# Gated attention in half chunks of 64 tokens with a middle state, four shared PSUM banks and a new order of the work

## The chip, the core and the metric

The kernel runs on one core of a Trainium2 chip. The core has five engines that work side by side, each strictly in its own order: TensorE multiplies matrices (its weight loads have a row of their own in the trace, PEld), VectorE (DVE) does elementwise work, ScalarE (ACT) applies functions and copies, GpSimd (POOL) and SyncE (SP) mostly issue transfers. TensorE writes its results to PSUM, which has eight banks of 2 KB in each of 128 partitions. The metric is the device time of one execution in microseconds, as the median of several.

## What is computed

For each of 4 x 8 heads a state of 48 x 48 complex numbers runs through 768 tokens: it is multiplied by a complex decay for each token and row, the outer product of `k` and `v` is added, and the output is `q` times its real part. A feed-forward block follows.

```python
def _attn_ref(q, k, v, a_re, a_im):
    ...
    for t in range(S):
        ar, ai = (a_re_n[:, :, t, :, None], a_im_n[:, :, t, :, None])
        new_re = ar * S_re - ai * S_im
        new_im = ar * S_im + ai * S_re
        kv = np.einsum('bhd,bhe->bhde', k[:, :, t], v[:, :, t])
        S_re, S_im = (new_re + kv, new_im)
        y[:, :, t] = np.einsum('bhd,bhde->bhe', q[:, :, t], S_re)

def _moe_ref(x, w_in, w_out):
    h = x @ w_in
    g = h * (1.0 / (1.0 + np.exp(-h)))
    return g @ w_out
```

`x` is the attention's output as 3072 x 384, `w_in` is 384 x 2048 and `w_out` 2048 x 384. The decay's size is capped at 0.999.

## The kernel before

The tokens are cut into 24 chunks of 128, numbered `n` from 0 to 23: four batches by six places in the sequence. Chunk `n` hands its state on to chunk `n + 4`, and the last four chunks hand on nothing. Two chunks form a pair `p`, twelve in all, and a pair's 256 tokens go through the feed-forward block together.

The recurrence of a chunk is done with matmuls. Two running sums over its tokens (`phases`, `summed`; in the order below `phase:n` and `L:n`) give the angle and the logarithm of the decay; sine, cosine and exponential follow on ScalarE. VectorE multiplies `k` and `q` by decay and rotation (`K`, `Q`), so that each head has 96 rows, a real and an imaginary part of 48. They are turned so that these 96 lie on the partitions: `squared` (`tk`, `tq`) transposes blocks of 32 x 32 on VectorE, and `homed` (`td`) moves the blocks home with 12 transfers, six on SP's queue and six on POOL's, into the tile `T`. Then per chunk:

- `weights` (`w:n.0`, `w:n.1`, line 613): for each head the product of all 128 keys with all 128 queries, four heads to a bank, into `a`.
- `masked` (`m`, line 626): VectorE multiplies each of the two banks with a triangle of ones, so that a query sees no later key, and writes `w`.
- `output` (`y:n`, lines 645 and 648): for each head the masked products times `v`, and from chunk 4 on `q` times the state `S`, added up in one bank. A head has 48 columns of weights but 64 are loaded, and even and odd heads go to the lower and the upper 64 partitions.
- `put` (`x:n`, lines 689 and 693): ScalarE copies the bank to `xT` and the last part of it to `y3`.
- `state` (`s:n`, line 716 from chunk 6 on): the chunk's own sum of `k` times `v`. It lies the wrong way round, so `state_squared` (`ss`, line 723) transposes it in blocks into `ssq` and `state_homed` (`sd`, line 734) moves it home with 12 transfers. `carried_on` (`S`, lines 749 and 751) adds the old state, multiplies by the whole chunk's decay `dec` and hands the result on.

The feed-forward block is `hidden` (`h:p.j`, lines 766, 776, 783), `silu` (`g`), the split of its result into parts (`gr`, `gb`, `gc`) and `result` (`r:p.j`, lines 968, 986, 1004). Its weights stand in three parts whose products make up for a lower precision; some parts are read again from memory for each pair (`lv`, `lw`).

A list of about 2,000 words such as `y:6` sets the order: each word is one step, and the steps' instructions go to their engines in that order. Nothing is reordered afterwards. PSUM has two banks for `phase`, `L`, `a`, `y` and `s` in turn, two for `h` in turn, and four for the block's results `o`.

## Time and profile before

| | |
|---|---|
| median of 3 runs | 606.78 us (606.25 to 607.14) |
| span of the profiled execution | 603.4 us |
| TensorE, matmuls | 583.3 us, 97% of the span |
| TensorE, weight loads | 509.3 us, 84% |
| VectorE | 495.7 us, 82% |
| ScalarE | 441.2 us, 73% |
| POOL | 222.5 us, 37% |

The span reaches from the first instruction of the program to the last; what lies around it makes up the difference to the run's time. Busy times of different engines overlap. A matmul's end is modelled, so what one costs is read from the starts of the records that follow each other, not from its duration. An fp32 matmul leaves two records.

### The profile page before, as it was taken

To read this page: it belongs to the slowest core of one execution; us is meant where nothing else is said; L and a number is where in the kernel's file an instruction comes from. 1 tells how busy PE (TensorE), PEld (TensorE's weight loads), DVE (VectorE), ACT (ScalarE), POOL (GpSimd) and SP (SyncE) were. 2 spreads that over 40 slices of the span, in tenths; PEclk is the share of its full clock that TensorE was granted. 3 is DMA by queue.
4 is the path that set the end of the run, shared out by engine and by line. 5 is a ranking of instruction groups with operands and counts; after the bars stand their busy time and mean duration, and the time that the engine had idled before them with its cause. 6 is when DMAs were issued, how large, how long until landed. Compare 5 with 4: busy or idle time off the path is not lost. (4 is left out here: it accounts for less than half of the span.)

```text
span 603.4 us, 11507 instructions
## 1 busy us (share of the span) xinstructions
PE 583.3 (97%) x3828; PEld 509.3 (84%) x3828; DVE 495.7 (82%) x765; ACT 441.2 (73%) x695; POOL 222.5 (37%) x389
## 2 busy tenths in 40 slices
PE   8588999999999999999999999999999999999997
PEld 6367877787767998998898898998898898999996
DVE  5899999987998989989889888889878786654644
ACT  7999999889885698896898895897884552342332
POOL 6364543636231534554444441536720323000000
PEclk9589999999999999999999999999999999999999
DMA  8988688977869977777868777859768467445652
GB/s 177 253 186 197 181 195 185 224 195 174 224 206 265 216 187 185 161 152 209 193 162 210 162 158 204 174 147 211 151 169 245 141 183 205 147 155 172 210 184 83
DMA packets 167728, 112.23 MB, mean 186 GB/s; under 512 B 137724, under 2 KB 143424, under 8 KB 167664
## 3 DMA queue, kind: packets, MB, share of 16 engines
q1 hardware_dynamic: 151920, 89.69, 57.2%
q0 software_dynamic: 12288, 17.23, 14.4%
q10 hardware_dynamic: 3456, 4.52, 2.1%
q8 instruction: 32, 0.52, 0.4%
q14 instruction: 32, 0.26, 0.2%
HBM read 81.14 MB, written 11.47 MB: 153 GB/s over the span
## 5 line engine op out<-in xcount | busy, mean ns | idle before, releaser
L307 ACT ACT_TABLE_LOAD x69 | 88.5, 1283 | 2.3 <-ACT ot L1017 0.8
L313 ACT ACTIVATE g<-h 128x512 f32<-128x512 f32 x96 | 56.0, 593 | 46.0 <-PE h L783 23.9
L600 POOL DMA_DIRECT2D T<-sq x120 | 70.1, 609 | 31.1 <-PE a L613 10.6
L944 ACT ACTIVATE head<-g 128x512 fp32r<-128x512 f32 x75 | 47.2, 630 | 46.2 <-PE o L986 25.9
L888 DVE SCALAR_TENSOR_TENSOR tail<-g,head 128x512 fp32r<-128x512 f32 x75 | 51.3, 683 | 32.1 <-ACT head L944 16.7
L528 POOL DMA_DIRECT2D dec<-ends x48 | 32.7, 722 | 117.6 <-DMA ends<-eq 116.8
L986 PE MATMUL o<-coarse,head 128*128 128x384 f32 x256 | 57.1, 344 | 0.5 <-ACT ot L1017 0.5
L766 PE MATMUL h<-xL,fine 128*128 128x512 f32 x192 | 55.3, 396 | 0.4 <-DMA fine<-w_firsts 0.4
L766 PE MATMUL h<-xD,mixed 128*128 128x512 f32 x192 | 55.2, 396 | 0.4 <-DVE xD L892 0.3
L986 PE MATMUL o<-diff,gd 128*128 128x384 f32 x256 | 55.4, 337 | 0.0
L892 DVE TENSOR_TENSOR gd<-tail,g 128x512 fp32r<-128x512 f32 x75 | 51.5, 687 | 4.3
L734 POOL DMA_DIRECT2D S<-ssq x84 | 46.8, 601 | 16.2 <-DVE ssq L723 10.3
L613 PEld LDWEIGHTS a<-T 96*128 96x128 f32 x384 | 49.9, 196 | 2.6 <-ACT T L605 0.3
L613 PE MATMUL a<-T 96*128 96x128 f32 x384 | 51.7, 281 | 0.1
L986 PEld LDWEIGHTS o<-coarse,head 128*128 128x128 f32 x256 | 44.8, 188 | 4.1 <-issue 1.1
L986 PE MATMUL o<-fine,tail 128*128 128x384 f32 x224 | 48.0, 336 | 0.0
L986 PEld LDWEIGHTS o<-diff,gd 128*128 128x128 f32 x256 | 45.5, 188 | 0.2 <-DVE gd L892 0.2
L776 PE MATMUL h<-xT,w 128*128 128x256 f32 x192 | 43.7, 381 | 1.6 <-ACT xT L689 1.6
L766 PEld LDWEIGHTS h<-xD,mixed 128*128 128x128 f32 x192 | 35.7, 188 | 10.1 <-DVE xD L892 1.2
L766 PEld LDWEIGHTS h<-xL,fine 128*128 128x128 f32 x192 | 36.0, 188 | 9.4 <-DMA fine<-w_firsts 0.8
L968 PE MATMUL o<-w,g 128*128 128x384 f32 x128 | 43.5, 488 | 0.0
L776 PEld LDWEIGHTS h<-xT,w 128*128 128x128 f32 x192 | 36.0, 190 | 7.9 <-ACT xT L689 1.8
(182 smaller groups left out, 1400.1 us busy)
## 6 DMA issues: line engine op xcount, KB each, us to landing
fine<-w_firsts SPq DMA_DIRECT2D x40, 384.0 KB
diff<-w_diffs SPq DMA_DIRECT2D x40, 384.0 KB
T<-sq SPq DMA_DIRECT2D x120, 64.0 KB
T<-sq POOLq DMA_DIRECT2D x120, 64.0 KB, 3.6
small<-in_moe_w_in_dram SPq DMA_DIRECT2D x16, 384.0 KB
raw<-in_moe_w_out_dram SPq DMA_DIRECT2D x16, 384.0 KB
small<-in_moe_w_out_dram SPq DMA_DIRECT2D x16, 384.0 KB
raw<-in_moe_w_in_dram SPq DMA_DIRECT2D x24, 192.0 KB
```

Of the source, the lines that this page charges most:

```text
L307: nc.scalar.preload_act_table_set(SETS[of][0])
L313: nc.scalar.activation(out=out, in_=in_, func=func, **kw)
L600: (nc.gpsimd if a % 2 else nc.sync).dma_start(out=to[ts(b, Q), :, a], in_=X[n]["sq"][ts(a, Q), b].rearrange("p w h x -> p (w h) x"))
L613: nc.tensor.matmul(ps[:, h], lhsT=x["kT"][hh * HH + h], rhs=x["qT"][hh * HH + h], start=True, stop=True)
L734: (nc.gpsimd if g % 2 else nc.sync).dma_start(out=to[ts(b, Q), r, :, e], in_=sq[ts(g, Q), :, b, 0:e.stop - e.start])
L766: nc.tensor.matmul(ps, lhsT=w[:, dc, ts(p % 2, C)], rhs=x[:, :, dc], start=(f == 0 and dc == 0), stop=(f == len(forms) - 1 and dc == ND - 1))
L776: nc.tensor.matmul(ps[:, ji], lhsT=of_first(w1, dc, jp * 2 + ji), rhs=A[p]["xT"][:, dc], start=(dc == 0), stop=(dc == ND - 1))
L888: nc.vector.scalar_tensor_tensor(out=dst, in0=whole, scalar=MORE / FINER, in1=head.bitcast(F32), op0=ALU.mult, op1=ALU.subtract)
L892: nc.vector.tensor_tensor(out=dst, in0=tail, in1=whole, op=ALU.subtract)
L944: nc.scalar.mul(g_form(p, jp, "head"), A[p]["g", jp], MORE * SPLIT / FINER)
L968: nc.tensor.matmul(A[p]["o"][m].rearrange("p n c -> p (n c)"), lhsT=A[p]["g", jp][:, ji, ts(m, C)], rhs=w2[jp][:, ji], start=(j == 0), sto ...
L986: nc.tensor.matmul(A[q_]["o"][m].rearrange("p n c -> p (n c)"), lhsT=left[:, i, ts(m, C)], rhs=right, start=(first_ and n == 0), stop=(las ...
```

## The change

From chunk 6 on (`n >= FULL`) a chunk is treated as two halves of 64 tokens.

- `weights_in_halves` (`wa`) forms only the two blocks on the diagonal, 64 keys by 64 queries: 16 matmuls for 8, each with half the weight columns and half the moving columns. The halves go to the lower and upper 64 partitions, so all eight heads fit one bank, and one mask on VectorE (`ma`) replaces two.
- What queries of the second half see of the first half comes from a state in the middle of the chunk. `state_of_pairs` now forms a sum for each half, over 64 tokens, into two banks. Both are transposed (`ss`) and moved home (`sd`), 12 transfers of twice the size, into a tile `new` with a single buffer. `middle` (`Sm`) adds the old state to the first sum on VectorE. The last four chunks need the first sum alone, where they had none before.
- `output` becomes two steps: `output_of_states` (`ys`) multiplies `q` of the first half by `S` and `q` of the second half by the middle state; `output_of_values` (`yv`) adds the masked products times `v`, contracting over 64 tokens. Each half has a bank of its own. `put` copies from two banks.
- `carried_on` adds both sums and writes the new state over the old one. `ssq` takes the buffer of `qr`.
- The running sum for `L` is no longer halved by its matrix; the exponential halves it by its scale.
- Four banks are shared by all users but `o`: each step takes the bank that was given back longest ago.
- The order is a new one throughout, not only where steps were replaced.

```diff
+class Banks:
+    def __init__(self, pool, n):
+        self.pool, self.free, self.of = pool, list(range(n)), {}
+    def tile(self, shape, dtype, *, name):
+        b = self.free.pop(0)
+        t = self.pool.tile(shape, dtype, tag=f"bank{b}", name=name, bufs=1)
+        self.of[name] = b
+        return t
+    def give(self, name):
+        self.free.append(self.of.pop(name))
...
-    p_m = Ring(fast.enter_context(tc.tile_pool(name="p_m", bufs=1, space=PSUM)), 2)
-    p_h = Ring(fast.enter_context(tc.tile_pool(name="p_h", bufs=1, space=PSUM)), 2)
+    banks = Banks(fast.enter_context(tc.tile_pool(name="p_b", bufs=1, space=PSUM)), 4)
...
+    def weights_in_halves(n):
+        x = X[n]
+        ps = banks.tile([C, H, SUB], F32, name=f"a{n}")
+        for h in range(H):
+            for i in range(2):
+                nc.tensor.matmul(ps[ts(i, SUB), h], lhsT=x["kT"][h][:, ts(i, SUB)],
+                                 rhs=x["qT"][h][:, ts(i, NA // 2)], start=True, stop=True)
+        x["a"] = ps
...
+    def outputs(n, left, right):
+        ps, first = output_banks(n)
+        for hp in range(HH):
+            for i in range(2):
+                for r in range(2):
+                    h = 2 * hp + r
+                    m = 64 if h + 1 < H else D
+                    nc.tensor.matmul(ps[i][64 * r:64 * r + m, hp], lhsT=left(i)[:, ds(h * D, m)],
+                                     rhs=right(i, h), start=first and hp == 0,
+                                     stop=not first and hp == HH - 1)
...
+    def output_of_states(n):
+        x = X[n]
+        s = [t.rearrange("p h d -> p (h d)") for t in (x["S"], x["new"][:, 0])]
+        outputs(n, lambda i: s[i], lambda i, h: x["qT"][h][:, ts(i, NA // 2)])
...
+    def output_of_values(n):
+        x = X[n]
+        outputs(n, lambda i: x["all v"][ts(i, SUB)], lambda i, h: x["w"][ts(i, SUB), h])
...
     def state_of_pairs(n):
-        ps = p_m.tile([C, HH, D2], F32, tag="m", name=f"s{n}")
-        for h in range(H):
-            hp, r = divmod(h, 2)
-            nc.tensor.matmul(ps[64 * r:64 * r + 64, hp], lhsT=x["all v"][:, ds(h * D, 64)],
-                             rhs=x["kr"][:, h].rearrange("p c d -> p (c d)"),
-                             start=True, stop=True)
+        x["ps"] = [banks.tile([C, HH, D2], F32, name=f"s{n}_{i}") for i in range(sums_of(n))]
+        for hp in range(HH):
+            for i, ps in enumerate(x["ps"]):
+                for r in range(2):
+                    h = 2 * hp + r
+                    nc.tensor.matmul(ps[64 * r:64 * r + 64, hp],
+                                     lhsT=x["all v"][ts(i, SUB), ds(h * D, 64)],
+                                     rhs=x["kr"][ts(i, SUB), h].rearrange("p c d -> p (c d)"),
+                                     start=True, stop=True)
...
+        new = X[n]["new"] = att.tile([D2, 2, H, D], F32, tag="new", name=f"new{n}", bufs=1)
...
+    def middle(n):
+        x = X[n]
+        mid = x["new"][:, 0]
+        nc.vector.tensor_tensor(out=mid, in0=mid, in1=x["S"], op=ALU.add)
...
-                v:8 turn:9 G5:5 g:1.7 ws:0 w:7.0 m:7.0 x:6 w:7.1 wk:3 wk:2 m:7.1 G1:5 wk:0 k:9 tk:8
...
+                phase:9 yv:6 x:6 hl:9 r:0.5 ul:9 ends:8 ws:3 K:8 wd:4 Sm:7 wq:5 wd:5 wk:3 G0:5 g:1.7
+                q:8 wa:7 wq:6 ma:7 last:8 k:9 ws:5 lv:2.0 r:0.6 wd:6 ys:7 yv:7 dq:8 x:7 G5:5 r:1.6
```

Three places show how instructions move. The first is TensorE at chunk 7. Before, `a` of the chunk is followed at once by its output; `T_1668` is the chunk's `T`, `S_829` its state, and the output's pattern goes on for 14 more rows:

```order
L648 MATMUL y_1722<-T_1455,S_756 48x128
L613 MATMUL a_0_1748<-T_1668 128x128 x4
L613 MATMUL a_1_1759<-T_1668 128x128 x4
L645 MATMUL y_1779<-w_0_1753,v_1327 64x128
L648 MATMUL y_1779<-T_1668,S_829 64x128
```

In the changed kernel it reads as follows, from the end of `ys` of chunk 6 (`T_1410`) to the start of `ys` of chunk 7 (`T_1637`); `new_1559` and `new_1711` are their middle states, in the same buffer:

```order
L681 MATMUL y_1_1684<-T_1410,new_1559 48x64
L483 MATMUL phase_1736<-th_parts_1611,upto_r 128x384 x2
L681 MATMUL y_0_1683<-w_1554,v_1404 64x64 x2
...
L1055 MATMUL o_0_943<-w_5_93,g_5_1439 128x384 x2
L1055 MATMUL o_1_944<-w_5_93,g_5_1439 128x384 x2
L656 MATMUL a_1793<-T_1637 64x64 x16
L1055 MATMUL o_0_943<-w_6_94,g_6_1607 128x384 x2
L1055 MATMUL o_1_944<-w_6_94,g_6_1607 128x384 x2
L681 MATMUL y_0_1826<-T_1637,S_767 64x64 x2
L681 MATMUL y_1_1827<-T_1637,new_1711 64x64 x2
```

The two `ys` are a phase, `yv` of chunk 6, two steps of `result` and `wa` of chunk 7 apart.

The second place is VectorE at the same point of the changed kernel: L819 is `middle`, L830 and L836 are `carried_on`, L663 is the mask.

```order
L819 TENSOR_TENSOR new_1559<-new_1559,S_708 96x384
L936 SCALAR_TENSOR_TENSOR fine_1701<-coarse,w_1_89 128x768
L979 TENSOR_TENSOR diff_1703<-coarse,mixed 128x768
L830 TENSOR_TENSOR new_1559<-new_1559 96x384
L836 TENSOR_TENSOR S_708<-new_1559,dec_1280 96x384
...
L936 SCALAR_TENSOR_TENSOR fine_1776<-coarse,w_4_92 128x768
L819 TENSOR_TENSOR new_1711<-new_1711,S_767 96x384
L936 SCALAR_TENSOR_TENSOR fine_1780<-coarse,w_5_93 128x768
L663 TENSOR_TENSOR w_1811<-a_1793,halves 128x512
```

Before, VectorE does the two masks of chunk 7 here in a row, and the state of chunk 6 is carried on some thirty rows later:

```order
L892 TENSOR_TENSOR diff_1746<-coarse,mixed 128x768
L626 TENSOR_TENSOR w_0_1753<-a_0_1748,upto_r 128x512
L626 TENSOR_TENSOR w_1_1766<-a_1_1759,upto_r 128x512
L594 STREAM_TRANSPOSE sq_1775<-kr_1634 128x3x4x2x32
L849 SCALAR_TENSOR_TENSOR fine_1777<-coarse,w_4_95 128x768
```

So the state's sums moved ahead of the masks and into the chain from chunk to chunk. On SP's queue the six transfers of chunk 7's sums stand between two stores of `w_diffs`, with a load of `q` and then `k` and `fine` behind:

```order
L1006 DMA w_diffs<-diff_1703 128x768
L813 DMA new_1711<-ssq_1675 32x8x32 x6
L1006 DMA w_diffs<-diff_1726 128x768
L547 DMA ends<-eq_1653 1x384
L1006 DMA w_diffs<-diff_1772 128x768
L197 DMA q_1791<-in_q_dram 128x8x48
```

The third place is ScalarE early on, ahead of the third and fourth copy into `xT`. Before:

```order
L307 ACT_TABLE_LOAD
L313 ACTIVATE mag_662<-mag_662 128x768
L605 COPY T_697<-tp_0_788 96x512
L307 ACT_TABLE_LOAD
L313 ACTIVATE g_1_814<-h_1_712 128x512
L248 ACTIVATE r<-raw 128x384
L307 ACT_TABLE_LOAD
L313 ACTIVATE eq_866<-L_833 128x384
L313 ACTIVATE L_865<-L_833 128x384
L248 ACTIVATE r<-raw 128x384
L307 ACT_TABLE_LOAD
L313 ACTIVATE g_0_872<-h_0_777 128x512
```

In the changed kernel, from the last table load ahead of the same copies:

```order
L324 ACT_TABLE_LOAD
L330 ACTIVATE g_0_816<-h_0_619 128x512
L330 ACTIVATE g_2_826<-h_2_819 128x512
L330 ACTIVATE g_3_837<-h_3_802 128x512
L263 ACTIVATE r<-raw 128x384 x3
L330 ACTIVATE g_1_871<-h_1_727 128x512
L330 ACTIVATE turn_893<-phase_878,round_b 128x384
```

Steps that need the same table now stand together. Up to the fourth copy into `xT` there are 12 table loads before and 8 now; on the path that runs, 70 before and 62 now.

## Rows read from the trace of the kernel before

**Rows 1.** The page's first part: busy us, share of the span, instructions.

```profile
PE 583.3 (97%) x3828; PEld 509.3 (84%) x3828; DVE 495.7 (82%) x765; ACT 441.2 (73%) x695; POOL 222.5 (37%) x389
```

**Rows 2.** Long stretches: length, busy PE, PEld, DVE, ACT, POOL, clock, DMA share, GB/s.

```profile
0.00:60.00 60.00, 45.75 (x305) 35.05 (x306) 50.80 (x98) 55.47 (x90) 32.23 (x58) 0.86 0.91 204
60.00:165.00 105.00, 105.00 (x653) 82.93 (x652) 96.14 (x151) 94.75 (x144) 49.38 (x77) 1.00 0.79 196
165.00:195.00 30.00, 29.14 (x144) 21.08 (x143) 27.90 (x37) 21.38 (x34) 8.00 (x14) 1.00 0.82 234
195.00:525.00 330.00, 329.54 (x2218) 296.75 (x2218) 279.66 (x416) 245.39 (x387) 132.93 (x240) 1.00 0.75 182
```

**Rows 3.** Timeline of TensorE, 307 to 314 us, merged: start, us, what.

```profile
307.53 2.04 PE L613 MATMUL a<-T 96*128 96x128 f32 x16
309.32 0.94 PE L986 MATMUL o<-coarse,head 128*128 128x384 f32 x4
310.10 0.86 PE L986 MATMUL o<-fine,tail 128*128 128x384 f32 x4
310.81 0.86 PE L986 MATMUL o<-diff,gd 128*128 128x384 f32 x4
311.59 0.88 PE L716 MATMUL s<-kr,v 128*64 128x96 f32 x16
312.30 0.44 PE L645 MATMUL y<-w,v 128*64 128x128 f32 x4
312.52 0.44 PE L648 MATMUL y<-T,S 96*64 96x128 f32 x4
...
313.85 0.44 PE L648 MATMUL y<-T,S 96*64 96x128 f32 x4
314.21 0.44 PE L986 MATMUL o<-coarse,head 128*128 128x384 f32 x1
```

**Rows 4.** The same from 311.5 us on: the last record ahead of `s`.

```profile
311.33 0.33 PE L986 MATMUL o<-diff,gd 128*128 128x384 f32 x1
```

**Rows 5.** Timeline of TensorE from 180 us: `s` without `y` behind it.

```profile
180.31 0.88 PE L716 MATMUL s<-kr,v 128*64 128x96 f32 x16
181.12 1.21 PE L613 MATMUL a<-T 96*128 96x128 f32 x8
```

**Rows 6.** Timeline of TensorE from 345.4 us: last `a` record, then `y`.

```profile
345.22 0.28 PE L613 MATMUL a<-T 96*128 96x128 f32 x1
345.44 0.43 PE L645 MATMUL y<-w,v 128*64 128x128 f32 x3
```

**Rows 7.** Timeline of VectorE at the same place, 343 to 347 us.

```profile
344.60 0.69 DVE L626 TENSOR_TENSOR w<-a,upto_r 128x512 f32<-128x512 f32 x1 [0.50 <-PE a L613]
345.54 0.69 DVE L626 TENSOR_TENSOR w<-a,upto_r 128x512 f32<-128x512 f32 x1 [0.25 <-PE a L613]
```

**Rows 8.** Groups by line and shape: busy us, mean ns, then idle time before.

```profile
L307 ACT ACT_TABLE_LOAD x69 | 88.5, 1283 | 2.3 <-ACT ot L1017 0.8 <-ACT ot L1011 0.4
L968 PE MATMUL o<-w,g 128*128 128x384 f32 x128 | 43.5, 488 | 0.0
L689 ACT COPY xT<-y 128x384 f32<-128x384 f32 x24 | 11.4, 473 | 17.9 <-PE y L648 17.6 <-PE h L776 0.2
L723 DVE STREAM_TRANSPOSE ssq<-s 128x384 f32<-128x384 f32 x14 | 8.1, 577 | 1.8 <-PE s L716 1.7
L693 ACT COPY y<-y 112x128 f32<-112x128 f32 x20 | 5.4, 270 | 0.0
L749 DVE TENSOR_TENSOR S<-S,S 96x384 f32<-96x384 f32 x14 | 7.6, 544 | 0.0
```

**Rows 9.** Line 734, the transfers of the sums: duration min/median/max, and landing.

```profile
L734 POOL DMA_DIRECT2D S<-ssq x84: 548/550/1170, 137.3 to 431.0; - x84
DMA to landing us min/median/max: 1.7/3.6/5.6
```

More of the change, by code (lines that the diff above doesn't have):

```diff
@@ L282 @@
     keep(ones, [[1, C]], 0, -1)
-    upto_r, half_r = (consts.tile([C, C], F32R, name=x) for x in ("upto_r", "half_r"))
+    upto_r = consts.tile([C, C], F32R, name="upto_r")
     nc.gpsimd.tensor_copy(out=upto_r, in_=ones)
-    nc.gpsimd.tensor_scalar(out=half_r, in0=ones, scalar1=0.5, scalar2=None, op0=ALU.mult)
-    upto, half = upto_r.bitcast(F32), half_r.bitcast(F32)
+    upto = upto_r.bitcast(F32)
+    halves = consts.tile([C, SUB], F32, name="halves")
+    for i in range(2):
+        nc.gpsimd.tensor_copy(out=halves[ts(i, SUB)], in_=ones[ts(i, SUB), ts(i, SUB)])
     one_b = consts.tile([C, 1], F32)
@@ L470, in phases @@
         x = X[n]
-        ps = p_m.tile([C, DM], F32, tag="m", name=f"phase{n}")
+        ps = banks.tile([C, DM], F32, name=f"phase{n}")
         running(ps, n, "th", upto, upto_r)
@@ L483, in turn @@
                                        op0=ALU.subtract, op1=ALU.add)
+        banks.give(f"phase{n}")
     def heads(t):
@@ L505, in summed @@
         first = n < STRAIGHT
-        ps = (p_o if first else p_m).tile([C, DM], F32, tag="o" if first else "m", name=f"L{n}")
-        running(ps, n, "l", upto if n < 2 else half, half_r)
+        ps = (p_o.tile([C, DM], F32, tag="o", name=f"L{n}") if first else
+              banks.tile([C, DM], F32, name=f"L{n}"))
+        running(ps, n, "l", upto, upto_r)
         x["L"] = ps
@@ L519, in decays @@
         x["decay"] = x["eq"]
-        special(x["eq"], x["L"], AF.Exp)
-        special(x["ek"], x["L"], AF.Exp, scale=-1.0)
+        whole = 1.0 if n < 2 else 0.5
+        special(x["eq"], x["L"], AF.Exp, scale=whole)
+        special(x["ek"], x["L"], AF.Exp, scale=-whole)
+        if n >= STRAIGHT:
+            banks.give(f"L{n}")
     def ends_of(n):
@@ L627, in masked, with masked_in_halves, output_banks @@
                                 in1=upto.unsqueeze(1).to_broadcast([C, HH, C]), op=ALU.mult)
+        banks.give(f"a{n}_{hh}")
+    def weights_in_halves(n):
[6 more added lines that the diff above has]
+        x["a"] = ps
+    def masked_in_halves(n):
+        x = X[n]
+        x["w"] = att.tile([C, H, SUB], F32, tag="w", name=f"w{n}", bufs=2)
+        nc.vector.tensor_tensor(out=x["w"], in0=x["a"],
+                                in1=halves.unsqueeze(1).to_broadcast([C, H, SUB]), op=ALU.mult)
+        banks.give(f"a{n}")
+    def output_banks(n):
+        x = X[n]
+        first = "y" not in x
+        if first:
+            x["y"] = [banks.tile([C, HH, SUB], F32, name=f"y{n}_{i}") for i in range(2)]
+        return x["y"], first
+    def outputs(n, left, right):
+        ps, first = output_banks(n)
+        for hp in range(HH):
+            for i in range(2):
+                for r in range(2):
[9 more added lines that the diff above has]
+    def output_of_values(n):
+        x = X[n]
+        outputs(n, lambda i: x["all v"][ts(i, SUB)], lambda i, h: x["w"][ts(i, SUB), h])
     def output(n):
@@ L688, in put @@
         ps = X[n]["y"]
-        nc.scalar.copy(out=A[p]["xT"][:, :, ts(i, C)], in_=ps[:, 0:ND])
-        if n >= STRAIGHT:
-            if "y3" not in A[p]:
-                A[p]["y3"] = att.tile([64 + D, T], F32, tag="y3", name=f"y3_{p}", bufs=1)
-            nc.scalar.copy(out=A[p]["y3"][:, ts(i, C)], in_=ps[0:64 + D, ND])
+        if n >= STRAIGHT and "y3" not in A[p]:
+            A[p]["y3"] = att.tile([64 + D, T], F32, tag="y3", name=f"y3_{p}", bufs=1)
+        parts = [(ps, ts(i, C), f"y{n}")] if n < FULL else [
+            (ps[k], ts(2 * i + k, SUB), f"y{n}_{k}") for k in range(2)]
+        for of, at, name in parts:
+            nc.scalar.copy(out=A[p]["xT"][:, :, at], in_=of[:, 0:ND])
+            if n >= STRAIGHT:
+                nc.scalar.copy(out=A[p]["y3"][:, at], in_=of[0:64 + D, ND])
+            banks.give(name)
     def state(n):
         x = X[n]
-        if place(n)[1] == NCH - 1:
-            return
         if n >= FULL:
@@ new lines @@
+                L:4 exp:4 v:3g k:4g F: F: H: H: q:5g k:6g s:3 S:3 R: t:3.1 J: J: G3:2 G6:2 G9:2 G8:2
+                im:6g thirds:3 q:4g w:2.1 t:3.2 T:3.2 h:0.3 T:3.1 m:2.1 Ga:2 H: g:0.0 h:0.2 g:0.2
+                dk:4 F: carried:4 w:3.0 g:0.3 im:7g ends:4 H: w:3.1 carried:5 m:3.0 R: J: m:3.1 H:
+                R: R: J: F: F: g:0.1 dq:4 L:5 re:7g phase:4 y:3 rd:4 turn:4 re:6g F: F: trig:4 K:4
+                y:2 last:4 phase:5 Q:4 x:3 H: tq:4 tk:4 J: r:0.0 R: R: x:2 G0:3 G5:3 J: H: J: G1:3
```

335 lines of the change are left out of this document (170 added, 165 removed).

## The prediction

> **What bounds the kernel now.** I began with busy time by engine: TensorE 97% of the span, VectorE 82%, ScalarE 73% [rows 1]. An average hides stages, so next came four long stretches [rows 2]. From 60 to 525 us TensorE is busy for all but 0.9 + 0.5 us; whatever its instructions take there is the time of the kernel. In the first 60 us it is busy for only 45.75, while ScalarE is busy for 55.47: there the end is set by ScalarE and VectorE, which prepare the first chunks. From 195 to 525 us VectorE has 279.66 of 330 us, 85%, so it has 50 us of room, but it works strictly in its order. A merged timeline of TensorE then gives the prices. One fp32 matmul leaves two records, so eight heads of `a` are 16 records.
>
> **TensorE's work before**, for chunks 6 to 23, the eighteen that change. `a` takes 1.79 us, from 307.53 to the next group at 309.32; `y` takes 1.91, from 312.30 to 314.21 [rows 3]. `s` takes 0.71 where `y` follows (311.59 to 312.30) [rows 3] and 0.81 alone (180.31 to 181.12) [rows 5]; of 14 chunks with an `s`, 6 have `y` behind it. Going from full-width to half-width weights costs 0.08: 311.33 to 311.59 is 0.26, where such a record takes 0.71 / 4 = 0.18 [rows 3, 4]. Coming back costs 0.14: the last four `y` records take 0.36 to the next group where others take 0.22 [rows 3]; this lies inside the 1.91 and the 0.81. The old order goes in 24 times. Sum: 18 x 1.79 + 18 x 1.91 + 6 x 0.71 + 8 x 0.81 + 24 x 0.08 = 32.2 + 34.4 + 10.7 + 1.9 = 79.2 us.
>
> **Its work after.** Four `y` records with 64 weight columns and 128 moving columns start over 0.22 us, so two of them, in the two column halves of the array, share 0.11 us [rows 3]. A full-width `a` record with 128 moving columns costs 1.79 / 16 = 0.11 by itself. Column halves therefore run side by side, at 0.00086 us per moving column; `s` with 96 columns fits (8 pairs x 0.083 = 0.66 of its 0.71). With 64 moving columns a pair should cost 0.055; I take 0.057. The upper bound is the 0.089 that a pair of `s` costs whole, since a load of 64 weight columns is hidden at 96 columns and no row shows it hidden at 64.
>
> `wa` and `ys`: 18 x 2 x 16 pairs x 0.057 = 32.8 us.
>
> `yv` and `s` now contract over 64 tokens, so two row halves and two column halves can hold four matmuls. No row before has a half of the rows. Side by side, `yv` is 18 x 8 fours at 0.055, 7.9 us; one row half after the other it is 288 pairs at 0.057, 16.4. I take 0.066 a four, 9.5 us, near the first, because column halves did run side by side and the two row halves write to different banks. `s` is 14 x 8 fours and 4 x 8 pairs (the last four chunks had no `s` before): 11.9 us at 0.083, 21.1 without row halves; taken 12.5.
>
> Switches: the new order enters half-width work 34 times, 34 x 0.22 = 7.5 us. Inside these runs it goes 21 times between half columns and quarters. No row shows that; between 0 and 0.22 each I take 0.14, 2.9 us.
>
> Sum 65.2, so **14.0 us less work**; bounds 20 less (0.055, fours side by side, free inner switches) and 33 more (0.089 for each pair, no row halves). [...]
>
> **What lies beside it.** VectorE: one mask of 0.69 us [rows 7] in place of two, 18 x 0.69 = 12.4 us less; 18 more transposes of 0.577 and 18 additions for the middle state at 0.544 [rows 8], 20.2 us more; net 8 us, within its 50 us of room. ScalarE: each chunk has two pairs of copies in place of one; from 0.473 for 384 and 0.270 for 128 columns [rows 8] half sizes cost 0.321 and 0.220, 18 x 0.34 = 6.1 us more. Against that the new order has 62 table loads for 70 on this path, 8 x 1.283 = 10.3 us less [rows 8]. Both are hidden by TensorE after 60 us. The last four chunks add 6 transfers on each of POOL's and SP's queues, 24 x 0.55 = 13 us of issuing [rows 9]; POOL is busy for 133 of 330 us there [rows 2], so I cost them at nothing beside the chain below. Shared banks remove no wait after 60 us, since there was none to speak of.
>
> **The start.** Up to the fourth copy into `xT` the new order has 8 table loads where the old has 12: 5.1 us of ScalarE in a stretch that ScalarE fills to 55.47 of 60 us [rows 2, 8]. VectorE is not relieved there (50.80 of 60). Between 0 and 6 us of TensorE's idle time can go; I take 3.
>
> **New waits.** *Chunk 7.* The buffer `new` is single and the state `S` is updated in place. So the sum of chunk 6 (`S:6`) waits for `ys:6` on TensorE, the transfers `sd:7` wait for `S:6`, the middle state `Sm:7` for the transfers, and `ys:7` for that. Price: 0.32 us from TensorE to VectorE (last `a` record at 345.22, its mask at 345.54) [rows 6, 7], two operations 1.1, six issues x 0.55, landing 3.6 [rows 9], addition 0.55 [rows 8], back 0.15: 9.0 us. Between `ys:6` and `ys:7` TensorE has a phase 0.36, `yv` 0.5, two results of four records at 0.340 [rows 8], `wa` 0.9, and three switches 0.66: 5.1 us. So TensorE waits 3.9 us. Behind `sd:7` on SP's queue stand the stores of `w_diffs` and the loads of `k`, `q` and `fine`; they are needed later than that. Elsewhere the same chain has 8.5 us (22 to 23), 9 (14 to 15, 18 to 19) or over 11 us of other work between; 0 to 3 each in the three short ones.
>
> *Masks.* Of the old kernel's masks the first starts while the second half of `a` runs, and `y` begins 0.22 us after the last `a` record has started [rows 6]. Now the one mask starts when all of `wa` is done: 0.32 + 0.69 + 0.15 (a mask ends at 345.29, `y` starts at 345.44) = 1.16 us, against 0.91 + 0.08 of `ys` between them. Seven chunks (9, 10, 13, 17, 19, 20, 23) have only `ys` there: 0.2 us each if VectorE stands ready, up to 0.9 more behind another operation. I take 3 us (1.4 to 7.7). The other chain waits, and VectorE at a few per cent more load over less time, together 3 us (0 to 8).
>
> **Sum.** -14.0 - 3 + 3.9 + 3 + 3 = -7.1 us. The span profiled is 603.4; the median run of 606.78 has 3.4 us around it, which nothing here touches. Forecast 606.8 - 7.1 = **599.7 us**.
>
> **Rivals.** *Row halves take turns* (slower). `yv` and `s` cost pairs, 37.5 us in place of 22.0: 615.2. For it: no row shows two row halves at once. Against: column halves do run at once. It decides the sign where the two together pass 29.1 us, about half way. Chance 0.12.
>
> *Weight loads come to light.* With 64 columns to stream, a pair stays at 0.089: `wa` and `ys` 51.3, `yv` and `s` 12.8 each, 22 us more: 621.8. Against: at 96 columns a load is hidden entirely [rows 3]. Chance 0.06. [...]
>
> *Waits eat the gain.* Masks 6, chunk 7 and its like 10, start only 2: 606.8 - 14 + 14 = 606.8. For it: every chunk's state now hangs on a chain of 9 us. Chance 0.16.
>
> *All of it comes in.* Work 18 less, start 5, waits 5: 588.8. Chance 0.20.
>
> **How the numbers follow.** The forecast itself, 594 to 605, has 0.46. Leaving out the lower half of the best case and most of the two slow ones gives 589 to 614. A difference under about 0.2% (1.2 us) cannot be told from none here. Faster by more: nearly all of the forecast, the best case and a quarter of the third rival, 0.68; within: 0.08; slower: 0.24.
>
> **What would show it.** `wa` and `ys` at about 0.9 us each and `yv` at 0.55 in TensorE's timeline (0.9 for `yv` would be the first rival, 1.4 for `wa` the second); `s` at about 0.75. A gap of some 4 us before `ys` of chunk 7, put down to `new`; gaps of a few tenths before `yv`, put down to `w`. TensorE's busy time in the first 60 us about 3 us higher. I am wrong if TensorE's gaps after 60 us add up to more than 15 us, or if VectorE becomes what ends most of them.

## The result, and the profile after

The changed kernel takes **612.93 us** (median of 7 runs, 608.92 to 616.98) where the kernel before takes 606.78 (7 runs beside it): ratio **1.0105**, 95% interval 1.0069 to 1.0140. It is slower by 1%; the forecast was 599.7, faster by 1.2%. The time lies inside the range of 589 to 614 and on the wrong side of 606.8.

The page's first part after the change, in the form of [rows 1]:

```profile
PE 577.1 (94%) x4980; PEld 493.9 (81%) x4980; DVE 502.8 (82%) x783; ACT 432.9 (71%) x723; POOL 239.1 (39%) x414
```

The long stretches, in the form of [rows 2]:

```profile
0.00:60.00 60.00, 46.43 (x319) 37.57 (x320) 48.97 (x95) 52.33 (x88) 31.08 (x57) 0.89 0.78 172
60.00:165.00 105.00, 100.16 (x669) 76.06 (x667) 93.22 (x150) 86.50 (x136) 48.67 (x76) 0.98 0.86 201
165.00:195.00 30.00, 27.54 (x216) 19.42 (x217) 27.06 (x37) 22.58 (x36) 10.70 (x19) 1.00 0.85 242
195.00:525.00 330.00, 322.90 (x3156) 282.16 (x3155) 285.65 (x428) 244.89 (x416) 145.50 (x259) 0.99 0.83 189
```

TensorE's busy time fell by 6.2 us, from 583.3 [rows 1], and the span rose by 7.8, from 603.4 to 611.2. TensorE now stands still for 4.8 us between 60 and 165 and for 7.1 between 195 and 525, where it stood still for 0 and 0.5 [rows 2]. The data engines' share between 195 and 525 rose from 0.75 to 0.83.

TensorE's timeline after, from 342.9 us: eight records in the middle of a `ys`, two `wa` in one piece (x64 are two chunks of 32 records), `yv`, and the first four records of the next `ys`.

```profile
342.92 0.29 PE L681 MATMUL y<-T,S 96*64 96x64 f32 x4
343.03 0.29 PE L681 MATMUL y<-T,new 96*64 96x64 f32 x4
...
348.57 2.23 PE L656 MATMUL a<-T 96*64 96x64 f32 x64
350.74 0.97 PE L1073 MATMUL o<-coarse,head 128*128 128x384 f32 x4
...
353.03 0.69 PE L681 MATMUL y<-w,v 64*64 64x64 f32 x32
353.65 0.34 PE L681 MATMUL y<-T,S 96*64 96x64 f32 x4
```

Two `wa` start over 2.17 us (348.57 to 350.74), 1.08 each; `yv` takes 0.62, from 353.03 to 353.65. Four records of `ys`, two pairs, start over 0.117 us, 0.0585 a pair, well under the 0.089 of a pair of `s` [rows 3] that was my upper bound: two 64-column matmuls do run side by side in column halves, with their weight loads hidden. The 32 records of `yv` would be 16 such pairs, 0.94 us, if one row half followed the other; without the 0.14 for the way back they take 0.48, so four run in the four quarters. The first two rivals are out.

To see where the rest went I laid every record of TensorE to its step of the order. For each kind of step (and for what kind follows it) I took the lower quartile of its length as its price and called the rest of its length waiting; slow clocks fall under waiting too. In us:

| | before | after | measured | forecast |
|---|---|---|---|---|
| steps that changed, chunks 6 to 23, with switches | 79.4 | 67.7 | -11.7 | -14.0 |
| waiting, 0 to 60 us | 22.4 | 19.2 | -3.2 | -3 |
| waiting, 60 to 150 us | 4.2 | 11.2 | +7.0 | 0 |
| waiting, 150 to 525 us | 9.4 | 21.0 | +11.6 | +9.9 |
| waiting, after 525 us | 0.1 | 1.5 | +1.4 | 0 |
| all other steps | 478.8 | 480.6 | +1.8 | 0 |

The sum is +6.9; the 1 us that is left of the span's rise lies behind TensorE's last record. The spans rose by more than the medians (6.1 us): in every run on record that has both, the span is 1.7 to 1.9 us shorter than the time, so the 603.4 before belong to a run of about 605.2 (an estimate), under the median. The work came in, with 2.3 us missing. The gain was eaten by waits (slow clocks among them), and the list of TensorE's waits (engine, line, releaser: us in total, times, longest) names other ones than the prediction did:

```profile
PE s L772 <- DVE kr L580: 5.2, 1, 5.2
PE phase L480 <- DVE th L453: 4.9, 2, 4.0
PE h L862 <- DVE S L836: 2.8, 1, 2.8
...
PE phase L483 <- ACT th_parts L467: 2.0, 1, 2.0
PE s L788 <- issue: 1.9, 1, 1.9
PE a L634 <- ACT g L330: 1.6, 2, 1.0
...
PE o L1073 <- DVE tail L975: 1.2, 2, 0.9
PE h L852 <- DMA fine<-w_firsts: 1.1, 1, 1.1
PE h L852 <- ACT g L330: 0.9, 1, 0.9
```

The first two lie in the first 29 us, where the kernel before has the same two at 3.3 and 3.1. Behind them stand four kinds. A shared bank that another step still holds (`h` for `S` of chunk 3; `a` and `h` for `g`, 2.5 us). Data that comes late: `fine`, and `th_parts`, which itself waited 4.1 us for the transfer `th<-last`. VectorE (`tail`). And 1.9 us in which TensorE waited for nothing that the profile shows.

The longest of them cost twice. Stretches around two waits (columns as above, the clock third from the end):

```profile
62.90:66.00 3.10, 0.33 (x4) 0.08 (x2) 1.65 (x4) 1.66 (x3) 0.00 (x0) 0.91 1.01 316
66.00:70.00 4.00, 4.00 (x12) 3.33 (x13) 3.97 (x7) 3.84 (x6) 1.69 (x3) 0.64 0.57 172
...
372.30:374.70 2.40, 0.41 (x3) 0.01 (x1) 0.02 (x1) 0.57 (x2) 0.70 (x2) 1.00 1.05 310
374.70:378.00 3.30, 3.15 (x9) 2.41 (x10) 2.94 (x5) 2.85 (x7) 0.00 (x0) 0.71 0.43 102
```

TensorE stands still for 2.8 and 2.0 us, and behind that the granted clock is 0.64 and 0.71: in slices of half a us it is 0.50 from 65.5 to 68.5 and from 376.2 to 379.2, and 1.00 again at 69.0 and at 379.5. The twelve records of `h:0.3` take 4.10 us there, 2.59 elsewhere, 1.5 more; after the second wait `h:7.2` takes 1.3 more. Both waits lie beside data engines that are full (shares 1.01 and 1.05).

### The profile page after: what moved, and what is told of

Read it like the earlier page. It is cut to its first block, busy times and chain, and to the rows that moved or that the text cites. A ratio compares the mean times of both kernels' runs of the same rounds, so it can differ in the third digit from the quotient of the medians.

```text
span 611.2 us, 14093 instructions
## 1 busy us (share of the span) xinstructions
PE 577.1 (94%) x4980; PEld 493.9 (81%) x4980; DVE 502.8 (82%) x783; ACT 432.9 (71%) x723; POOL 239.1 (39%) x414
## 5 line engine op out<-in xcount | busy, mean ns | idle before, releaser
L813 POOL DMA_DIRECT2D new<-ssq x108 | 62.9, 589 | 55.0 <-DVE ssq L798 21.2
L550 POOL DMA_DIRECT2D dec<-ends x48 | 31.2, 660 | 83.0 <-DMA ends<-eq 67.2
L862 PE MATMUL h<-xT,w 128*128 128x256 f32 x192 | 45.0, 390 | 2.8 <-DVE S L836 2.8
L852 PE MATMUL h<-xH,firsts 128*128 128x512 f32 x144 | 42.3, 402 | 0.0
L979 DVE TENSOR_TENSOR mixed<-firsts,fine 128x768 fp32r<-128x768 f32 x30 | 28.5, 950 | 14.3 <-PE h L869 6.2
```

The costliest lines, as they stand in the source:

```text
L550: nc.gpsimd.dma_start(out=x["dec"][a * D:(a + 1) * D], in_=ends[n].rearrange("(h d) -> d h", d=D))
L813: (nc.gpsimd if g % 2 else nc.sync).dma_start(out=to[ts(b, Q), r, :, e], in_=sq[ts(g, Q), :, b, 0:e.stop - e.start])
L852: nc.tensor.matmul(ps, lhsT=w[:, dc, ts(p % 2, C)], rhs=x[:, :, dc], start=(f == 0 and dc == 0), stop=(f == len(forms) - 1 and dc == ND - 1))
L862: nc.tensor.matmul(ps[:, ji], lhsT=of_first(w1, dc, jp * 2 + ji), rhs=A[p]["xT"][:, dc], start=(dc == 0), stop=(dc == ND - 1))
L979: nc.vector.tensor_tensor(out=dst, in0=tail, in1=whole, op=ALU.subtract)
```

## The experiments

Each ratio is to the kernel before on the same chip, with its 95% interval. My theory after the traces: two separate losses, a start in which VectorE falls behind, and transfers in the middle that come too late. Its rivals: shared banks, VectorE's load, and waits that only change their name.

**The banks alone.** The old kernel and its order, with the four banks shared.

```diff
-    p_m = Ring(fast.enter_context(tc.tile_pool(name="p_m", bufs=1, space=PSUM)), 2)
-    p_h = Ring(fast.enter_context(tc.tile_pool(name="p_h", bufs=1, space=PSUM)), 2)
+    banks = Banks(fast.enter_context(tc.tile_pool(name="p_b", bufs=1, space=PSUM)), 4)
```

> The kernel before with one edit: its four banks for phases, weights, results of attention, states and hidden layers are shared by need (the bank longest free is taken next) where they were two rings of two. Order and work are the old ones. If the sharing itself costs (in the changed kernel TensorE waited 2.8 us for a bank that the state sum of chunk 3 held, 2.5 us in all for banks that silu held), it comes out 3 to 6 us slower than 606.8, with waits of h or a on S or g. If the sharing costs only through the new order, it stays within 1.2 us of 606.8: in the old order a bank was free in time anyway.

607.68 us, 1.0016 (1.0001 to 1.0031): 1 us, hardly more than nothing. What sharing costs beyond that comes only with the new order, where a step takes a bank that is still held.

**The start, both ways.** `old_start` gives the changed kernel the old list's first 447 words, up to 125 us; the attention of chunks 4 and 5 then reads a state that is already carried on, since the new kernel updates it in place. `old_start_apart` has these states in places of their own. `new_start` gives the old kernel with shared banks the new list's first 312 words, up to 85 us. `old_first` gives the changed kernel the old list's first 79 words only.

```diff
-re:0 warm:20 im:0 im:1 e0:0 e1:0 e2:0 re:1g e0:1 e1:1 warm:34
+re:0 im:0 hold: e0:0 warm:34 re:1g e1:0 re:2g e2:0 e4:0 e0:1
...
+m:4.0 w:5.1
```

> The changed kernel whose order follows the old kernel up to the fourth chunk's attention (the first 125 us, where both work with whole chunks), then its own. If the start is where the loss sits (62.6 us: a wait of 2.9 us and then slow matmuls, about 4.5 us; banks held by silu 1.9 us), it comes out 4 to 6 us faster than the changed kernel, 607 to 609. If the loss sits behind 125 us (late transfers), it gains 0 to 2 us: 611 to 613.

> The old order up to 125 us and then the new one, as before, with the states of chunks 4 to 9 in places of their own, so that the old order's early state sums disturb nothing. Same work and places on TensorE: 608.5 to 610 if the 609.15 of that run was a matter of order alone; a gain beyond that would have to come from the removed dependence of sums on results of attention in the first chunks, of which TensorE shows no wait.

> The other way round: the old program with shared banks, in the new order up to 85 us (312 of its 1911 words), then in the old order. If the new start is slower by itself, whatever follows, it comes out 2 to 5 us slower than the old program with shared banks (607.7): 610 to 613. If the new start is only slower because of what follows it, 606 to 608.5.

> The changed kernel in the old order for the first 29 us alone (79 words; one sum before the first transposes), then in its own. In those 29 us ScalarE waited 3.4 us for loads of a_re in the new order and 1.6 in the old. If the first loads are where the new start loses, 2 to 4 us of the 4 to 7 come back: 608 to 611, with less spread. If it loses later (weights at 45 to 65 us, VectorE behind them), 612 to 615.

609.15 us, 1.0032 (1.0015 to 1.0048); 610.35, 1.0069 (1.0044 to 1.0093); 615.41, 1.0140 (1.0112 to 1.0167); 613.64, 1.0111 (1.0074 to 1.0148). The old start takes 2 to 4 us off the changed kernel, and the new start puts 7.5 us on the old one (1.0140 to 1.0016), so it is slower by itself, unless the place where the two orders are joined costs something, which no run tests. The trace of `new_start` is that of its shortest run (610.05); its span is only 2.3 us over that of `banks_only`. The old first 29 us alone give nothing back: the trace of `old_first` reaches `phase:10` at 196.5 us, the changed kernel's at 196.2. The new start loses in the stretch from 60 to 110 us, here of `old_start`, then the changed kernel, then `new_start` (columns as in [rows 2], VectorE's busy time the third figure behind the length):

```profile
60.00:110.00 50.00, 49.77 (x290) 39.59 (x290) 47.85 (x83) 46.90 (x71) 21.31 (x29) 1.00 0.77 190
```
```profile
60.00:110.00 50.00, 46.40 (x254) 35.88 (x253) 42.23 (x73) 41.40 (x65) 19.84 (x28) 0.97 0.87 198
```
```profile
60.00:110.00 50.00, 44.63 (x247) 34.12 (x248) 42.96 (x74) 40.13 (x62) 19.94 (x29) 0.97 0.84 200
```

With the old start VectorE is busy for 47 to 48 of these 50 us in every trace, with the new one for 40 to 43. No work of VectorE's was saved here, so by 110 us it is some 5 us behind.

**Single moves in the new start.** `s3_first` issues the state sum of chunk 3 ahead of two conversions of weights; `f_first` issues four fetches of weights earlier on SP's queue.

```diff
-H: H: q:5g k:6g s:3 S:3 R: t:3.1
+q:5g k:6g s:3 S:3 H: H: R: t:3.1
```
```diff
-R: R: rq:2.1 t:2.3 dk:3
+R: R: F: F: F: F: rq:2.1 t:2.3 dk:3
```

What stood behind them in the changed kernel, VectorE's timeline:

```profile
60.53 0.69 DVE L49 SCALAR_TENSOR_TENSOR w<-raw,w 128x512 int32<-128x512 int32 x1
64.31 0.43 DVE L47 TENSOR_SCALAR w<-raw 128x512 int32<-128x512 int32 x1 [3.09 <-DMA raw<-in_moe_w_in_dram]
64.77 0.69 DVE L49 SCALAR_TENSOR_TENSOR w<-raw,w 128x512 int32<-128x512 int32 x1
65.38 0.55 DVE L836 TENSOR_TENSOR S<-s,dec 96x384 f32<-96x384 f32 x1
```

> The changed kernel with one move in its order: the state sum of chunk 3 (S:3) is issued on VectorE ahead of two conversions of weights that wait for their transfers. If h:0.3 at 62.6 us waits for the bank of S:3 and nothing behind it, the 2.9 us go and with them the slow matmuls after it: 4 us faster than the changed kernel, about 609. If the weights that stand in front are what h:0.3 or its neighbours need next, the wait only gets another name: 612 to 613.

> The changed kernel with one move in its order: four fetches of weight blocks (the 8th to the 11th) stand on SP's queue right behind the conversions that free their buffers, ahead of the transfers of ends:2 and ends:3 that wait for ScalarE (in the changed kernel they were issued from 48.4 us on and the last landed at 64.3, where VectorE and ScalarE had waited 3 us each for it and TensorE 2.9). If the new start loses its time to this queue, both waits go and TensorE's slow matmuls behind them: 3 to 5 us faster, 607.5 to 610. If the data engines are full there anyway, 0 to 1 us: 611 to 613.

614.89 us, 1.0129 (1.0095 to 1.0164), and 614.50, 1.0133 (1.0103 to 1.0162): no gain. TensorE's waits between 55 and 75 us with `s3_first`, and between 40 and 75 with `f_first`:

```profile
PE h L862 <- DVE w L56: 1.2, 1, 1.2
PE s L772 <- DMA v<-in_v_dram: 0.7, 1, 0.7
```
```profile
PE s L772 <- DMA v<-in_v_dram: 2.7, 2, 1.4
```

The wait for `S` is gone from both, and the weights, or the loads of `v` that the fetches now stand ahead of, are late in its place. So neither word by itself is the cause. That the new start asks for more data and conversions around 60 us than come in is my reading of these waits; no run takes only this load away.

**The transfers in the middle.** `half_moved` leaves out part of the work: only the first half's sums are moved (its state adds that half twice). `light_traffic` does the same and loads only 32 of the 384 columns of the blocks that are looked at for small weights; the look then reads one column over and over, 384 numbers as before. `before_light` is the control, the old kernel with such loads. `late_looks` moves 29 of these 32 loads whole behind 525 us, and `both` adds the move of `f_first` to that.

```diff
-        to = new[:, 0:k].rearrange("p s (h r) e -> p r (s h) e", r=2)
+        to = new[:, 0:1].rearrange("p s (h r) e -> p r (s h) e", r=2)
```
```diff
-                out=raw.bitcast(I32), in_=w[:, ts(n % (NT // 2), DM)].bitcast(I32).rearrange(
+                out=raw[:, 0:32].bitcast(I32),
+                in_=w[:, ds(n % (NT // 2) * DM, 32)].bitcast(I32).rearrange(
...
```

> The changed kernel without one part of its work: the transfers that bring the transposed sums of a chunk home move only the first half's sum (the state then adds that half twice, so the output differs). As many transfers of half the size; all else as it was. If the doubled traffic (small packets under 512 bytes went from 105 thousand to 121 thousand between 195 and 525 us) makes th, fine, diff and TensorE's own instructions late, TensorE's waits there fall by 5 to 8 us: 605 to 608, and the spread of the runs shrinks. If traffic is not the cause, it stays at 611 to 614.

> The changed kernel with less traffic: only the first half's sums of a chunk are moved (as in the run before), and the blocks of weights that are loaded only to look for small numbers are loaded with 32 of their 384 columns (the look then reads one column as often). 32 loads of 384 KB shrink to a twelfth; the output differs. If the data engines' load makes th, fine, diff and T late, TensorE's waits between 150 and 525 us fall by 5 us or more: under 608. If these loads come late because of where their issue stands in a queue, the time stays within 2 us of the changed kernel's 611.5 to 613.

> The control: the kernel before with the looks' loads at 32 of 384 columns (the output is the same as long as no weight is tiny). If lighter traffic helps any order, it gains what the changed kernel gained, 4 to 6 us: 601 to 603. If the old order has room for its traffic, as its 1.2 us of waits for data in the middle say, it gains under 1.5 us: 605.5 to 607.

> The changed kernel with the 29 loads (384 KB each) that look for small weights from the third on moved to the last 80 us, one behind each step of TensorE there; 15 of them stood between 188 and 523 us. The same work and traffic, elsewhere. If traffic in the middle is what costs (the run with light traffic came out at 605.8), most of that gain comes: 606 to 608. If the end, where the data engines were busy for about 55%, cannot take them, the loads of diff and fine come late there: 610 to 613.

> The two moves together (four fetches earlier, the looks at the end). If they are separate losses they add up: 601 to 604, faster than the kernel before (606.9). If the start's loss is made good later anyway, 606 to 608.

611.53 us, 1.0072 (1.0050 to 1.0095), which can't be told from the changed kernel; **605.82, 0.9993** (0.9973 to 1.0013); 606.55, 0.9994 (0.9981 to 1.0006); 614.50, 1.0131 (1.0100 to 1.0162); 614.96, 1.0172 (1.0126 to 1.0217). Less traffic gives the changed kernel 7 us and the old kernel nothing. The stretch from 195 to 525 us, of `light_traffic`, of the control, of `half_moved` and of `late_looks`:

```profile
195.00:525.00 330.00, 327.01 (x3278) 288.31 (x3276) 291.38 (x437) 247.35 (x420) 144.78 (x261) 1.00 0.74 171
```
```profile
195.00:525.00 330.00, 329.16 (x2214) 295.87 (x2213) 279.18 (x414) 245.85 (x388) 132.63 (x239) 1.00 0.71 164
```
```profile
195.00:525.00 330.00, 322.91 (x3155) 283.30 (x3154) 285.57 (x427) 244.21 (x415) 142.82 (x258) 0.99 0.79 183
```
```profile
195.00:525.00 330.00, 326.12 (x3187) 286.22 (x3186) 284.48 (x422) 248.51 (x421) 149.92 (x265) 1.00 0.78 174
...
525.00:600.00 75.00, 72.09 (x572) 69.60 (x571) 46.57 (x77) 22.64 (x42) 1.48 (x3) 1.00 0.77 255
```

In the changed kernel and its kin with a share of 0.82 or 0.83 TensorE stands still for 6 to 9 of these 330 us; at 0.74 for 3.0, at 0.78 (`late_looks`) for 3.9, but in `half_moved`, at 0.79, still for 7.1. The old order stands still for 0.5 at 0.75 and for 0.8 at 0.71. So the share alone doesn't say how long.

These windows hold different work in different runs. The same steps lie between the starts of `phase:10` and `phase:23` in TensorE's timeline (us):

| | to `phase:10` | `phase:10` to `phase:23` | the rest |
|---|---|---|---|
| changed kernel | 196.2 | 296.8 | 118.3 |
| `half_moved` | 195.0 | 297.1 | 117.7 |
| `light_traffic` | 196.4 | 289.6 | 117.5 |
| `late_looks` | 198.6 | 292.5 | 121.6 |
| `less_vector` (below) | 197.1 | 291.1 | 118.7 |

The gain of `light_traffic` lies nearly all in the middle, and `half_moved` has none of it: what helps is the shrinking of the looks' loads, which the change left alone, and not the halving of the new transfers by itself. Where the looks go to the end, the middle gains 4.3 us and the end loses 3.3; up to `phase:10`, where the order is the same, this run was 2.4 us slower, and the time shows no gain.

**VectorE's load.** `less_vector` leaves out the middle state and all work on the second half's sums.

```diff
-        nc.vector.tensor_tensor(out=mid, in0=mid, in1=x["S"], op=ALU.add)
+        pass
...
```

> The changed kernel with less work for VectorE: the middle state isn't formed, and of a chunk's sums only the first half's are transposed, moved and carried on (the output differs). 18 additions of 0.55 us, 14 of the same kind for the sum of the halves and 14 transposes of 0.52 go, 25 us of VectorE, and the chain from one chunk's state to the next is one operation shorter. If VectorE's load is what makes TensorE wait between 150 and 525 us (some 12 us more than before the change), 6 to 10 us of these go: 603 to 607. If VectorE only carries the blame for transfers and for the order, 0 to 3 us go: 610 to 613.

609.30 us, 1.0060 (1.0034 to 1.0087): 3 to 4 us better than the changed kernel, between the 6 to 10 and the 0 to 3 that were expected, and too near `half_moved` (1.0072) to be told from it by its time. The trace says more. `phase:10` and `phase:23` start here in the changed kernel, then in this run:

```profile
196.16 0.51 PE L483 MATMUL phase<-th_parts,upto_r 128*128 128x384 f32 x2
492.92 0.51 PE L483 MATMUL phase<-th_parts,upto_r 128*128 128x384 f32 x2
```
```profile
197.12 0.51 PE L483 MATMUL phase<-th_parts,upto_r 128*128 128x384 f32 x2
488.17 0.51 PE L483 MATMUL phase<-th_parts,upto_r 128*128 128x384 f32 x2
...
195.00:525.00 330.00, 325.61 (x3186) 285.83 (x3184) 272.45 (x395) 247.77 (x421) 144.66 (x262) 1.00 0.80 184
```

The middle is 5.7 us shorter, where `half_moved`, whose lighter transfers are in this run too, has nothing. From 195 to 525 us TensorE stands still for 4.4 us at a share of 0.80, where it is 7.1 at 0.79 in `half_moved`. One trace is little, but six others (the changed kernel, `half_moved`, `old_first`, `s3_first`, `f_first`, `s10_later`) have 295.8 to 297.2 us there. So VectorE's load, or the chain that it stands in, can't be ruled out: taking it away gives back nearly as much of the middle as taking away the looks' loads.

**Longer runs in place of less data.** `long_T` interleaves the eight heads of k in T, so that a transfer moves runs of 1 KB where it moved 256 bytes; `before_long_T` is the control, and `old_start_long_T` has the old start as well.

```diff
-                k_ = [t[:, 0, h].rearrange("p a (j r) -> p (a j) r", r=2) for h in range(HH)]
-                x["kT"] = [k_[h // 2][:, :, h % 2] for h in range(H)]
...
+                k_ = t[:, 0].rearrange("p a (j h) -> p (a j) h", h=H)
+                x["kT"] = [k_[:, :, h] for h in range(H)]
...
```

> The changed kernel with another layout of T, the homes of k and q: the eight heads lie interleaved in a row of 256 numbers, so that the 12 transfers of a chunk move runs of 1 KB where they moved runs of 256 bytes. The same bytes, instructions and order; k's weights are read with a stride of 8 numbers where it was 2. Between 195 and 525 us the 24 thousand packets of 256 bytes took 667 us of the 16 engines' time, 12.6%. If the engines' load makes TensorE wait in the middle (12 us more than before the change), this gives what the light traffic gave, 4 to 7 us: 606 to 609. If the gain of the light run came from its missing issues or its missing second sums, 611 to 614.

> The control: the kernel before with the longer runs of T alone. Its order had 1.2 us of waits for data in the middle, and the light looks gave it 0.4 us. So 605.5 to 607. A loss beyond 1 us would mean that weights read with a stride of 8 numbers, or transposes written with it, are slower, and the other two runs would carry that too.

> All that the runs say is needed: the old order up to 125 us, the halves and the new order behind it, and T in longer runs. If the start (some 4 us) and the traffic (some 6) are separate losses, 602 to 605, faster than the kernel before (606.9). If the waits in the middle come back under another name, 606 to 609.

625.29 us, 1.0298 (1.0257 to 1.0340); 644.99, 1.0628 (1.0605 to 1.0650); 623.37, 1.0259 (1.0235 to 1.0282). The control shows why: reading k's weights at a stride of 8 numbers doubles `a` (one of its weight loads takes 310 ns there, 196 before). From `long_T`, two `wa` and the transposes that write k so:

```profile
357.42 4.08 PE L656 MATMUL a<-T 96*64 96x64 f32 x64
```
```profile
L616 DVE STREAM_TRANSPOSE sq<-kr 128x768 f32<-128x768 f32 x20 | 33.3, 1667 | 0.0
L616 DVE STREAM_TRANSPOSE sq<-qr 128x768 f32<-128x768 f32 x20 | 19.4, 972 | 0.3
```

4.08 us for what took 2.23, and 1667 ns for k where q, still in runs, takes 972. TensorE's idle time from 195 to 525 did fall, to 3.9 us at a share of 0.76, but `wa` is longer there too, so this run says nothing on the traffic by itself.

**Both losses relieved.** `old_start_light` is `old_start_apart` with the light traffic; it leaves out what `light_traffic` leaves out, by the same edits.

> The old order up to 125 us with states apart, the new one behind it, and the light traffic: only the first half's sums are moved, and the looks load 32 of 384 columns (the output differs in the carried state). If start and traffic are separate losses, their gains add up: 610 less 5 to 7, 602 to 605, and the 11 us of TensorE's work that the halves save show at last below 606.8. If the waits only go elsewhere, 606 to 609.

**602.00 us, 0.9908** (0.9884 to 0.9932). The two gains add up, so the losses are separate, and with both relieved the saved work shows: 5.4 us under the kernel before on the same chip (607.39), where the changed kernel is 6 above it. It isn't a kernel to use, since it moves only half of the sums; of those that do all the work none beat the kernel before.

**The gap without a releaser.** `s10_later` moves one step behind the next result.

```diff
-yv:9 v:10 s:10 G9:6 gc:2.4 lw:2.4 r:2.4 ss:10 sm:5
+yv:9 v:10 G9:6 gc:2.4 lw:2.4 r:2.4 s:10 ss:10 sm:5
```

> The changed kernel with s:10 and its transposes moved behind the result r:2.4, so that the 256 instructions of wa:9, ys:9, yv:9 and s:10 no longer stand in one piece. Within s:10 TensorE had stood still for 0.8 to 2.2 us in three profiles, with nothing to wait for, just after a 16 KB load of its own instructions. If its instructions come too late there, the gap is gone from s:10 or under 0.3 us; the time falls by 1 us at most, which is too little to measure: 611 to 614. If s:10 waits for something else, the gap stays where s:10 is.

616.06 us, 1.0104 (1.0069 to 1.0140), the time of the changed kernel. The same step in the changed kernel, then in this run:

```profile
230.95 0.66 PE L788 MATMUL s<-kr,v 64*64 64x96 f32 x18
233.52 0.56 PE L788 MATMUL s<-kr,v 64*64 64x96 f32 x14 [1.92 <-issue]
```
```profile
237.26 0.89 PE L788 MATMUL s<-kr,v 64*64 64x96 f32 x32
238.85 0.62 PE L483 MATMUL L<-l_parts,upto_r 128*128 128x384 f32 x2 [0.70 <-DVE ssq L798]
```

Behind `wa`, `ys` and `yv` the step breaks off in its middle; by itself it runs through. A queue of the page loads instructions by 16 KB (q8, part 3), 0.52 MB in 32 times before and 0.67 MB in 41 after. With TensorE's 3,828 and 4,980 records that is 120 and 121 to a load, so I take these for TensorE's instructions (an estimate). In the changed kernel one such load starts at 230.7 us and takes 1.07, to 231.8; the break begins at 231.6. In the traces of `old_start`, `old_first`, `old_start_light` and `half_moved` the same step breaks off for 1.4, 1.4, 1.2 and 0.8 us. Two traces in which the step stands as in the changed kernel (`s3_first`, `less_vector`) have less than 0.3 us there, so that the load causes it is not shown. The gain went at once into a wait for a bank (`ssq`).

## Why the prediction was wrong, step by step

The forecast had the span 7.1 us shorter; it was 7.8 longer. Of the 14.9 us between, 7.0 are waits from 60 to 150 us, which were in no term; 2.3 are missing work, 1.7 more waits in the middle than the 9.9 forecast, 1.4 waits behind it, 1.8 other steps, and 1 lies behind TensorE's last record. The first 60 us gave 0.2 more than forecast. The 3.4 us "around" the span were some 1.6 too many, since the run that was profiled lay that much under the median.

- **The work** was right in its mechanism and 2.3 us short in size: -11.7 for -14.0. A pair of 64 columns starts over 0.0585 us, not 0.057. Between `ys` and `yv` the switch costs about 0.18 (`ys` takes 1.12 ahead of `yv`, 16 pairs of it 0.94), where I took 0.14.
- **The start** is the first step that failed, and the largest. By the table TensorE waited 3.2 us less in the first 60 us, as forecast, but it is busy for only 0.7 us more there (46.43 for 45.75), where the sign I gave asked for 3; most of the rest would be the clock (0.89 for 0.86), which was in no term. Then it lost 7.0 by 150 us. I counted ScalarE's 5.1 us of saved table loads as time that the others could use. They became waits for data: up to 110 us ScalarE waits 8.6 us for transfers, before 1.6. It is busy for 93.7 us for 101.7, and VectorE, from which nothing was taken, for 91.2 where it had been busy for 98.5. I had read that VectorE was full there [rows 2] and asked only whether it is relieved, not whether the new order keeps it fed. The runs put this at 2 to 4 us seen from one side, 7.5 from the other.
- **The middle** is the second. I costed the new transfers "at nothing", by POOL's idle time, put VectorE's added work "within its 50 us of room", and kept 3 us for all waits but the masks and chunk 7. Those two cost 2 us at most (below), so about 10 fell to the others. That the sum of the middle's waits, 11.6, comes near my 9.9 is luck. What I did not ask is how much the data engines had left (0.75 of their time taken [rows 2]), nor see that each transfer of sums now carries two: 16 and 32 KB where it was 8 and 16. Packets between 195 and 525 us rose from 120,216 to 135,815, the share to 0.83, and the landing of `T<-sq` from 3.6 to 4.9 us. But that these bytes are what costs is not shown: halving the new ones gave the middle nothing (`half_moved`), and `less_vector` gains 5.7 us with `T<-sq` still landing in 4.9. What the runs show is an order with no slack. It gets most of its middle back when the looks' loads shrink, which the old order doesn't mind, and also when VectorE has less to do.
- **Chunk 7**, priced at 3.9 us, costs 0.9, and not at `ys:7`: `wa:7` waits for `T`. The timeline:

```profile
160.97 0.61 PE L483 MATMUL phase<-th_parts,upto_r 128*128 128x384 f32 x2
161.51 0.69 PE L681 MATMUL y<-w,v 64*64 64x64 f32 x32
162.13 2.85 PE L1055 MATMUL o<-w,g 128*128 128x384 f32 x8
165.38 1.56 PE L656 MATMUL a<-T 96*64 96x64 f32 x32 [0.40 <-DMA T<-sq]
166.87 2.85 PE L1055 MATMUL o<-w,g 128*128 128x384 f32 x8
169.65 0.34 PE L681 MATMUL y<-T,S 96*64 96x64 f32 x4
```

  From the last record of `ys:6` to `ys:7` there are 8.7 us, this wait among them, not 5.1: I gave each result four records where it has eight.
- **Masks**, priced at 3 us, cost about 1 at most: no wait of TensorE for a mask is among the rows above, and the eleven `ys` with `yv` right behind start over 1.03 to 1.45 us, in all 0.9 more than 1.12 each.
- **Shared banks** "remove no wait", I wrote, and did not ask whether they add one. In the old order they cost 1 us; in the new one they make `h:0.3` wait for a state sum, which itself stands behind a late transfer of weights.
- **A slower clock** was in no term. The two waits above brought 2.8 us of it.

The third rival, waits that eat the gain, is what happened, at 14 us of waits; they came to 16.8. It had the size right and the places wrong: its masks (6 us) and chunk 7 and its like (10) cost about 2, and its start, which was to gain 2, lost 3.8 up to 150 us. The sign of being wrong was met, just: from 60 to 600 us TensorE stands still for 15.1 us. It is not VectorE alone that ends these gaps.

Open: which of the start's transfers and conversions is the first to be late, since two single moves only renamed the wait; what binds the middle, the data engines, VectorE or the chain through both, since either relief helps and no run gives VectorE's share by itself; and the 3 us of standing still that remain at a share of 0.74, spread over banks, VectorE's `tail` and `xL`, and instructions.

## What to carry to other kernels

Before counting saved work on the bounding engine as time, look at what the other resources have left in the same stretch, the data engines' share beside the busy times, and ask of a new order whether each engine's inputs still arrive early. A stretch in which one engine is full, as VectorE is here in the first 110 us, is priced by whether the new order keeps that engine fed, and a loss there is seen in its busy time up to a fixed point. A control, the same relief given to the old kernel, tells a cause from a general gain. But a relief that helps doesn't name the cause: here two different ones each gave back most of the middle. And where time windows hold different work, compare the runs from one step to another.

## What the runs showed of the hardware

- Four matmuls of 64 rows by 64 columns run in the four quarters at once: `yv`'s 32 records take 0.62 us with the way back, where 16 pairs would take 0.94 (an estimate, 16 x 0.0585). Weight loads of 64 columns stay hidden behind 64 moving columns: a pair in column halves starts over 0.0585 us (`ys`).
- Weights read at a stride of 8 numbers (32 bytes) doubled a step that reads them at a stride of 2 before: four heads of `a` take 1.75 us in the control (`before_long_T`) where they take 0.85, and one of their weight loads 310 ns for 196; VectorE's transposes that write so take 1667 ns for 972.
- Packing small matmuls raises the count of instructions (TensorE's records rose from 3,828 to 4,980), and in a run of small ones, at the end of a load of instructions, TensorE broke off for 1.9 us with nothing to wait for (`s:10`, above); that the load is the cause is not shown.
- Two waits of 2.0 and 2.8 us each cost 1.3 and 1.5 us more in the lower clock behind them (0.71 and 0.64).
